# Attention products of two tiles at a time, in quarters of the array, in a fused attention and MLP kernel

## The chip, the cores and the metric

The kernel runs on one core of a Trainium2 chip. TensorE (PE in the profile) multiplies matrices out of on-chip memory into PSUM, which has eight banks. VectorE (DVE) and ScalarE (ACT) do elementwise work and read and write PSUM too; SyncE (SP) issues the DMAs. Each engine takes its instructions strictly in the order in which the program lists them, and waits at one whose inputs or whose buffer aren't ready; everything behind it on that engine waits too. The metric is the device time of one execution in microseconds (us); lower is better.

## The reference

Eight batches, eight heads, 576 rows, head size 64, all fp32. An attention without softmax, normalized by its root mean square for each head, then a two-layer MLP with a squared relu:

```python
kv  = np.einsum('bhsd,bhse->bhde', k, v)
out = np.einsum('bhsd,bhde->bhse', q, kv)
rms = np.sqrt(np.mean(out * out, axis=-1, keepdims=True) + 1e-06)
x   = (out / rms * g_norm)            # (B,H,S,D) -> (B*S, H*D): 4608 x 512
h   = x @ w_in                        # 512 x 2048
g   = np.maximum(h, 0.0) ** 2
y   = g @ w_out                       # 2048 x 512
```

The MLP is nearly all of the arithmetic. For each row the attention needs a product with a 64x64 matrix for each head.

## The kernel before

**Tiles and strips.** The 4608 rows of x are 36 tiles of 128. Two batches make nine tiles (`PAIR`): four of the even batch, one that holds the last 64 rows of both, four of the odd batch. Four tiles are a strip; nine strips, 0 to 8, are worked one after the other. `x_n[n]` is the normalized tile n, `xt[s]` the transposed strip, which feeds the MLP.

**The MLP.** The products of a strip are written as Strassen products (seven in place of eight block products). A strip's first half, `up`, has 28 steps: four groups g, each with products in the order 1, 2, 6, 5, 7, 3, 4. Each step is 8 records of L552 on TensorE. Results gather in three kinds of PSUM banks: A (two buffers) for 1, 6, 7, 4, B for 5, 3 and C for 2. After 1, 6 and 5 ACT copies the bank aside (`snap`, L562); product 6 goes on in the bank of product 1, product 7 in that of 6, product 4 in that of 7, and product 3 in that of 5, so each waits until the bank has been read. After 2, 7 and 3 DVE adds the snap to the bank and squares the relu (L611, L612); in strips 0 and 1 product 3 is followed by two more sums (`sums_g`, L579 and L241). After 4 ACT squares the relu. The second half, `down`, has 14 steps; from strip 2 on each product of it is itself a small Strassen product (L736). Strip 0 uses plain products in its first half (`up_first`, L588), beside which ACT and DVE convert the fp64 weights that arrive piece by piece (L203 to L224).

**Attention work.** It is cut into slices, kept in one list (`slices`, L487 to L512), which is what fixes its order. For each batch b: for each pair p of heads `transposed_query` and `key_value`, then for each tile `query` and, one place behind, `features` (batch 1) or `squares_x` (batches 2 to 7). `attend(n)` (L515) issues all slices up to place n. In strip s it is called after every step, with a place that grows in a straight line from `ready[s]` to `ready[s+1]` while the step weights (1 for a step of `up`, 2 for one of `down`, 56 in a strip from strip 2 on) reach 0.42 of their sum, so all slices of a strip fall into the first 24 steps of `up`. In strip 0 the slices of batch 1 fall one each on the last eight steps of `up_first` and the first six steps of `down`. Batch 0 comes ahead of everything, in `first_queries`, `first_normalized` and `first_features`.

- `key_value` (L342): 20 records on TensorE; the two heads of a pair stand in two halves of the array's columns. ACT copies the two 64x64 results into the diagonal of a 128x128 matrix `kvd[b, p]` with zeros elsewhere (L351, L352).
- `products_x` (L365): a query tile times `kvd`, four products of 128x128x128 into one bank; the mixed tile takes two halves of columns (L373).
- `mean_squares` and `inverse_root` (L381, L390): ACT squares the bank into `sq` (one buffer), DVE sums over each head and scales, ACT takes a root, DVE a reciprocal and one Newton step in three small instructions; `normalized` multiplies.
- `features` (L448): TensorE transposes a copied tile. `squares_x` (L456): DVE transposes squares of 32x32 straight out of PSUM, then SP stores to DRAM and loads four times into `xt`.
- PSUM: `apsum` has four buffers with the tag `at` for all of the attention, taken in turn; A, A, B, C have the other four banks.

Of the kernel before, what the change touches and what calls it, by code (L numbers as in the profile page):

```python
# [9 lines left out]
FP32 = mybir.dt.float32  # L10
# [3 lines left out]
AF = mybir.ActivationFunctionType  # L14
ALU = mybir.AluOpType
AX = mybir.AxisListType
# [3 lines left out]
def kernel(  # L20
# [34 lines left out]
    nc = tc.nc  # L55
    P = 128
    B, H, S, D = q.shape
    n_tok = B * S
    d_model = H * D
    d_ff = moe_w_in.shape[1]  # L60
    NP = H // 2
    FC = d_ff // P
    C = S // P
    REST = S - C * P
    PAIR = 2 * C + 1
    assert 2 * REST == P
    N_TILE = n_tok // P
    NT = 4
# [6 lines left out]
    X_ON_PE = 2  # L75
# [6 lines left out]
    xn_pool = ctx.enter_context(tc.tile_pool(name="xn", bufs=2))  # L82
# [4 lines left out]
    conv = ExitStack()  # L87
    raw_pool = conv.enter_context(tc.tile_pool(name="raw", bufs=8))
    wtmp = conv.enter_context(tc.tile_pool(name="wtmp", bufs=4))
    apsum = ctx.enter_context(tc.tile_pool(name="apsum", bufs=4, space=bass.MemoryType.PSUM))  # L90
    fpsum = ctx.enter_context(tc.tile_pool(name="fpsum", bufs=1, space=bass.MemoryType.PSUM))
    ctx.enter_context(tc.manual_schedule())

# [268 lines left out]

    by_head = lambda t: t.rearrange("p (h d) -> p h d", d=D)

    def products_x(n):  # L365
        m, c = divmod(n, PAIR)
        ps = apsum.tile([P, d_model], FP32, name="x_ps", tag="at")
        for p in range(NP):
            o = ps[:, ts(p, P)]
            if c == C:  # L370
                for h in range(2):
                    half = slice(REST * h, REST * (h + 1))
                    nc.tensor.matmul(  # L373
                        o[half], lhsT=qT["rest", m, p][:, half], rhs=kvd[2 * m + h, p], start=True, stop=True
                    )
            else:
                b, c_b = (2 * m, c) if c < C else (2 * m + 1, c - C - 1)
                nc.tensor.matmul(o, lhsT=qT[b, p][:, c_b, :], rhs=kvd[b, p], start=True, stop=True)  # L378
        return ps

    def mean_squares(ps):  # L381
        n = ps.shape[-1] // D
        sq = xn_pool.tile([P, d_model], FP32, name="sq", tag="sq", bufs=1)
        nc.scalar.activation(sq, ps, AF.Square)
        ms = small.tile([P, H], FP32, name="ms", tag="ms")
        nc.vector.reduce_sum(out=ms, in_=by_head(sq), axis=AX.X)
        nc.vector.tensor_scalar(out=ms, in0=ms, scalar1=1.0 / D, scalar2=EPS, op0=ALU.mult, op1=ALU.add)
        return ms

    def inverse_root(ms):  # L390
        r = small.tile([P, H], FP32, name="rms", tag="rms")
        nc.scalar.activation(r, ms, AF.Sqrt)
        nc.vector.reciprocal(r, r)

        t = small.tile([P, H], FP32, name="newton", tag="newton")
        nc.vector.scalar_tensor_tensor(out=t, in0=ms, scalar=-0.5, in1=r, op0=ALU.mult, op1=ALU.mult)
        nc.vector.tensor_tensor(out=t, in0=t, in1=r, op=ALU.mult)
        nc.vector.scalar_tensor_tensor(out=r, in0=t, scalar=1.5, in1=r, op0=ALU.add, op1=ALU.mult)
        return r

    def normalized(n, ps, r):

        on_pe = n < X_ON_PE * C + (X_ON_PE > 1)
        x_n[n] = xn_pool.tile([P, d_model], FP32, name="x_n", tag="x_n") if on_pe else ps
        nc.vector.tensor_tensor(
            out=by_head(x_n[n]), in0=by_head(ps), in1=r.unsqueeze(2).to_broadcast([P, H, D]), op=ALU.mult
        )

    def query(n):
        ps = products_x(n)  # L410
        normalized(n, ps, inverse_root(mean_squares(ps)))

    first = {}

    def first_queries(p):

        ps = apsum.tile([P, NT, P], FP32, name="x_ps", tag="at")
        for n in range(NT):
            nc.tensor.matmul(ps[:, n, :], lhsT=qT[0, p][:, n, :], rhs=kvd[0, p], start=True, stop=True)
        steps = conversion(p, w_in[:, p % KH, 0, p // KH * 2 : p // KH * 2 + 2])  # L420
        next(steps)
        next(steps)
        first[p] = flat(ps), mean_squares(flat(ps)), steps

    def first_normalized(p):
        ps, ms, steps = first.pop(p)
        next(steps)
        x_n["first", p] = t = xn_pool.tile([P, NT, P], FP32, name="x_n", tag="x_n")
        r = inverse_root(ms)
        nc.vector.tensor_tensor(  # L430
            out=by_head(flat(t)), in0=by_head(ps), in1=r.unsqueeze(2).to_broadcast([P, H, D]), op=ALU.mult
        )
        for _ in steps:
            pass

    def first_features(p):
        t, x = x_n.pop(("first", p)), open_xt(0)
        ps = apsum.tile([P, NT, P], FP32, name="xt_ps", tag="at")
        for n in range(NT):
            nc.tensor.transpose(ps[:, n, :], t[:, n, :], ident)  # L440
        nc.scalar.activation(x[:, :, p, :], flat(ps).rearrange("p (a t) -> p a t", t=SQ), AF.Copy, scale=g_col)
# [14 lines left out]
    def squares_x(n):  # L456

        s, i = divmod(n, NT)
        t, x = x_n.pop(n), open_xt(s)
        q = xn_pool.tile([P, 4, NP, SQ], FP32, name="x_q", tag="x_n")  # L460
        nc.vector.transpose(
            out=q.rearrange("p f q t -> p q f t"), in_=t.rearrange("p (q f d) -> p q f d", q=NP, f=4)
        )
        d = dram.tile([P, 4, NP, SQ], FP32, name="x_d", tag="x_d", bufs=4)
        nc.sync.dma_start(out=d, in_=q)
        for f in range(4):
            nc.sync.dma_start(
                out=x[ts(f, SQ), ts(i, 4)].rearrange("d a q t -> d a (q t)"),
                in_=d[:, f].rearrange("(a d) q t -> d a (q t)", a=4),
            )  # L470
# [17 lines left out]
    for b in range(B):  # L488
        for p in range(NP):
            if b:  # L490
                slices += [(transposed_query, (b, p)), (key_value, (b, p))]
                continue

            slices += [(convert_on_act, (p,)), (transposed_query, (b, p)), (key_value, (b, p))]
            if p > 0:
                slices.append((first_normalized, (p - 1,)))
            slices.append((first_queries, (p,)))
            if p > 0:
                slices.append((first_features, (p - 1,)))
        first_n = b // 2 * PAIR + (C if b % 2 else 0)  # L500
        ns = list(range(first_n, first_n + C + b % 2))
        if b == 0:
            slices += [(first_normalized, (NP - 1,)), (first_features, (NP - 1,))]
            ready[0] = len(slices)
            continue
        for i in range(len(ns) + 1):
            if i < len(ns):
                slices.append((query, (ns[i],)))
            if 0 < i <= len(ns):
                slices.append((features if b < X_ON_PE else squares_x, (ns[i - 1],)))  # L510
            if i > 0 and ns[i - 1] % NT == NT - 1:
                ready[ns[i - 1] // NT] = len(slices)  # L512
    slice_at = [0]

    def attend(n):  # L515
# [374 lines left out]
```

## Time and profile before

| what | us |
|---|---|
| median of 6 runs | 963.99 (963.38 to 964.73) |
| the profiled execution | 964.27 |
| its span in the trace | 962.5 |
| TensorE busy, matmul records | 928.5 (5976 records) |
| DVE busy | 644.4 |
| ACT busy | 229.0 |
| L378 x_ps, whole query tiles | 29.5 busy, 224 records |
| L373 x_ps, mixed tiles | 4.4 busy, 64 records |

A row of instruction groups gives the line, engine, operation, what is written and read, the shape and the number of records. One fp32 product appears as two records of matmul and two of weight load (PEld). A matmul record's duration includes the pipeline, and records overlap: what counts for the time is how far one start lies behind the other. The chain that ended last is followed back from the last instruction, at each step to what released it.

### The profile page before, as it was taken

The numbers are of one execution on the slowest core, as the hardware profiler recorded it, in microseconds if no ns is written. First come the engines' busy times: TensorE is split into PE (matmuls) and PEld (weight loads), VectorE is DVE, ScalarE is ACT, GpSimd is POOL, SyncE is SP. The second block draws the span as 40 slices with busy tenths as digits, with TensorE's granted clock in tenths as the row PEclk, the third lists the DMA queues.
The fourth block names the chain that finished last, engine by engine and source line by source line (L and its number), as shares of the span: only waits on it lengthen the run. The fifth ranks groups of instructions, "written<-read, shape, count | busy, mean of one in ns | idle before, by whom it ended". The sixth has DMA issues, their size and how long they took to land.

```text
span 962.5 us, 15319 instructions
## 1 busy us (share of the span) xinstructions
PE 928.5 (96%) x5976; PEld 816.7 (85%) x5976; DVE 644.4 (67%) x1161; ACT 229.0 (24%) x501; POOL 1.7 (0%) x7
## 2 busy tenths in 40 slices
PE   3699999999999999999999999999999999999996
PEld 3344888888888998899989998999889988998996
DVE  3899764585437875587648874786568655863583
ACT  3697441320023002210222012201320022002200
POOL 0000000000000000000000000000000000000000
PEclk9899999999999999999999999999999999999998
DMA  8699883636974585557564765467506721672064
GB/s 243 223 291 302 271 224 137 141 100 217 321 244 124 176 290 173 124 178 258 191 153 129 254 217 155 119 227 274 134 23 239 251 91 55 229 256 63 15 233 147
DMA packets 164520, 180.33 MB, mean 187 GB/s; under 512 B 85088, under 2 KB 138848, under 8 KB 155872
## 3 DMA queue, kind: packets, MB, share of 16 engines
q1 hardware_dynamic: 164288, 179.36, 59.0%
q8 instruction: 47, 0.77, 0.3%
q14 instruction: 25, 0.20, 0.1%
q10 hardware_dynamic: 160, 0.00, 0.0%
HBM read 148.11 MB, written 31.20 MB: 186 GB/s over the span
## 4 chain that ended last, share of the span: by engine, by line
PE 95%; ACT 2%; DVE 2%; DMA 1%; SPq 0%; issue 0%; DVEq 0%
PE ps_A L552 29%; PE ps_B L552 14%; PE ps_B L736 14%; PE ps_A L736 14%; PE ps_C L552 12%; PE ps_A L588 3%; PE x_ps L378 3%; PE kv_ps L349 2%; PE ps_B L588 1%; PE ps_C L588 1%; DMA raw<-in_moe_w_in_dram 1%; PE x_ps L373 0%; ACT raw L206 0%; ACT w_c L203 0%; PE xt_ps L440 0%
## 5 line engine op out<-in xcount | busy, mean ns | idle before, releaser
L552 PE MATMUL ps_A<-x_t,w_in 128*128 128x256 f32 x768 | 182.6, 381 | 1.3 <-DVE gt L611 1.3
L552 PEld LDWEIGHTS ps_A<-x_t,w_in 128*128 128x128 f32 x768 | 143.6, 190 | 21.1 <-DVE gt L611 2.1
L736 PE MATMUL ps_B<-w_blk,g_s 128*128 128x128 f32 x672 | 81.9, 275 | 0.0
L736 PE MATMUL ps_A<-w_blk,g_s 128*128 128x128 f32 x672 | 81.9, 275 | 0.0
L736 PEld LDWEIGHTS ps_B<-w_blk,g_s 128*128 128x128 f32 x672 | 78.4, 192 | 0.0
L736 PEld LDWEIGHTS ps_A<-w_blk,g_s 128*128 128x128 f32 x672 | 78.4, 192 | 0.0
L612 DVE SCALAR_TENSOR_TENSOR gt<-gt 128x512 f32<-128x512 f32 x96 | 66.4, 692 | 3.3
L562 ACT COPY snap<-ps_A 128x512 f32<-128x512 f32 x68 | 39.8, 585 | 113.8 <-PE ps_A L552 93.2
L611 DVE TENSOR_TENSOR gt<-ps_C,snap 128x512 f32<-128x512 f32 x32 | 22.0, 688 | 65.0 <-PE ps_C L552 65.0
L736 PE MATMUL ps_B<-w_blk,gt 128*128 128x128 f32 x504 | 63.1, 275 | 0.0
L736 PE MATMUL ps_A<-w_blk,gt 128*128 128x128 f32 x504 | 63.1, 275 | 0.0
L611 DVE TENSOR_TENSOR gt<-ps_A,snap 128x512 f32<-128x512 f32 x32 | 22.0, 688 | 60.0 <-PE ps_A L552 59.9
L552 PE MATMUL ps_A<-xT,w_in 128*128 128x256 f32 x256 | 61.2, 382 | 0.0
L552 PE MATMUL ps_C<-xT,w_in 128*128 128x256 f32 x256 | 61.0, 381 | 0.0
L552 PE MATMUL ps_B<-x_t,w_in 128*128 128x256 f32 x256 | 60.9, 381 | 0.0
L241 DVE TENSOR_TENSOR gt<-gt 128x2048 f32<-128x2048 f32 (+1 forms) x31 | 58.1, 1873 | 4.0 <-PE ps_C L552 3.8
L552 PE MATMUL ps_B<-xT,w_in 128*128 128x256 f32 x256 | 60.7, 380 | 0.0
L736 PEld LDWEIGHTS ps_A<-w_blk,gt 128*128 128x128 f32 x504 | 60.2, 192 | 0.4
L736 PEld LDWEIGHTS ps_B<-w_blk,gt 128*128 128x128 f32 x504 | 60.2, 192 | 0.4
L552 PE MATMUL ps_C<-w_blk,gt 128*128 128x256 f32 x256 | 56.6, 379 | 0.0
L552 PEld LDWEIGHTS ps_C<-xT,w_in 128*128 128x128 f32 x256 | 48.2, 190 | 6.7 <-issue 0.2
L552 PEld LDWEIGHTS ps_B<-xT,w_in 128*128 128x128 f32 x256 | 48.3, 190 | 6.5
(118 smaller groups left out, 1263.5 us busy)
## 6 DMA issues: line engine op xcount, KB each, us to landing
w_blk<-w_deep SPq DMA_DIRECT2D x42, 1024.0 KB, 5.3
w_blk<-w_out SPq DMA_DIRECT2D x42, 768.0 KB, 4.9
w_blk<-w_out SPq DMA_DIRECT2D x18, 1024.0 KB, 5.1
raw<-in_moe_w_in_dram SPq DMA_DIRECT2D x16, 512.0 KB, 6.5
raw<-in_moe_w_out_dram SPq DMA_DIRECT2D x16, 512.0 KB, 5.4
k<-in_k_dram SPq DMA_DIRECT2D x30, 256.0 KB, 2.9
v<-in_v_dram SPq DMA_DIRECT2D x30, 256.0 KB, 3.6
w_deep<-w_t SPq DMA_DIRECT2D x7, 1024.0 KB, 8.7
```

What stands on the lines that cost most here:

```text
L241: eng.tensor_tensor(out=out, in0=a, in1=b, op=ALU.subtract)
L349: nc.tensor.matmul(ps[ts(h, D)], lhsT=a, rhs=w, start=c == 0, stop=c == C)
L378: nc.tensor.matmul(o, lhsT=qT[b, p][:, c_b, :], rhs=kvd[b, p], start=True, stop=True)
L552: nc.tensor.matmul(bank[BANK[p]][:, i, :], lhsT=lhsT(k), rhs=rhs(k), start=p in (1, 5, 2) and i == 0 and k == 0, stop=k == n - 1, skip_gro ...
L562: nc.scalar.copy(snap[p], b)
L588: nc.tensor.matmul(ps, lhsT=w_in[:, kc % KH, g, kc // KH * 2 + fh, ts(i, P)], rhs=xt[0][:, :, kc, :], start=kc == 0, stop=kc == NP - 1,)
L611: nc.vector.tensor_tensor(out=o, in0=b, in1=a, op=ALU.add)
L612: nc.vector.scalar_tensor_tensor(out=o, in0=o, scalar=0.0, in1=o, op0=ALU.max, op1=ALU.mult)
L736: nc.tensor.matmul(chain[c][x][:, i, :], lhsT=a[:, f, :], rhs=w[:, f, :], start=p not in (6, 7, 3) and j in (1, 3) and f == 0, stop=f == F ...
```

## The change

`products_x` takes two tiles at once (the last tile of an odd batch alone). Every product is cut into four of 64x64x64: the rows of the array by the head's parity r, its columns by the halves of the tile's rows. So only the two nonzero 64x64 blocks of `kvd` are used. Even heads go into one bank, odd heads into another; tile i takes half of each bank. This two-bank tile has one buffer, tag `x`; `at` goes from four buffers to two, and the first queries and first features move into banks A, B and C.

`query` now holds the products and the mean squares of both tiles; `normalized` is a slice of its own with one root and one Newton step for both; then come the two `features` or `squares_x`. `squares_x` transposes in two instructions, one for each bank. With the longer list the slices move: tile 8's query goes from strip 0 into strip 1, and `ready` changes.

```diff
-    apsum = ctx.enter_context(tc.tile_pool(name="apsum", bufs=4, space=bass.MemoryType.PSUM))
+    apsum = ctx.enter_context(tc.tile_pool(name="apsum", bufs=2, space=bass.MemoryType.PSUM))
...
-    def products_x(n):
-        m, c = divmod(n, PAIR)
-        ps = apsum.tile([P, d_model], FP32, name="x_ps", tag="at")
+    def products_x(ns):
+
+        ps = apsum.tile([P, 2, 2, d_model // 2], FP32, name="x_ps", tag="x", bufs=1)
         for p in range(NP):
-            o = ps[:, ts(p, P)]
-            if c == C:
+            for i, n in enumerate(ns):
+                m, c = divmod(n, PAIR)
                 for h in range(2):
                     half = slice(REST * h, REST * (h + 1))
-                    nc.tensor.matmul(
-                        o[half], lhsT=qT["rest", m, p][:, half], rhs=kvd[2 * m + h, p], start=True, stop=True
-                    )
-            else:
-                b, c_b = (2 * m, c) if c < C else (2 * m + 1, c - C - 1)
-                nc.tensor.matmul(o, lhsT=qT[b, p][:, c_b, :], rhs=kvd[b, p], start=True, stop=True)
+                    if c == C:
+                        q, b = qT["rest", m, p], 2 * m + h
+                    else:
+                        b, c_b = (2 * m, c) if c < C else (2 * m + 1, c - C - 1)
+                        q = qT[b, p][:, c_b]
+                    for r in range(2):
+                        row = slice(D * r, D * (r + 1))
+                        nc.tensor.matmul(
+                            ps[half, r, i, ts(p, D)], lhsT=q[row, half], rhs=kvd[b, p][row, row], start=True, stop=True
+                        )
         return ps
 
-    def mean_squares(ps):
-        n = ps.shape[-1] // D
-        sq = xn_pool.tile([P, d_model], FP32, name="sq", tag="sq", bufs=1)
-        nc.scalar.activation(sq, ps, AF.Square)
-        ms = small.tile([P, H], FP32, name="ms", tag="ms")
-        nc.vector.reduce_sum(out=ms, in_=by_head(sq), axis=AX.X)
+    def mean_squares(parts):
+        ms = small.tile([P, 2, H], FP32, name="ms", tag="ms")[:, : len(parts)]
+        for i, ps in enumerate(parts):
+            sq = xn_pool.tile(list(ps.shape), FP32, name="sq", tag="sq", bufs=1)
+            nc.scalar.activation(sq, ps, AF.Square)
+            if len(ps.shape) == 3:
+                sq = sq.rearrange("p r e -> p (r e)")
+            nc.vector.reduce_sum(out=ms[:, i], in_=by_head(sq), axis=AX.X)
         nc.vector.tensor_scalar(out=ms, in0=ms, scalar1=1.0 / D, scalar2=EPS, op0=ALU.mult, op1=ALU.add)
         return ms
 
     def inverse_root(ms):
-        r = small.tile([P, H], FP32, name="rms", tag="rms")
+        r, t = (small.tile([P, 2, H], FP32, name=n, tag=n)[:, : ms.shape[1]] for n in ("rms", "newton"))
         nc.scalar.activation(r, ms, AF.Sqrt)
         nc.vector.reciprocal(r, r)
 
-        t = small.tile([P, H], FP32, name="newton", tag="newton")
         nc.vector.scalar_tensor_tensor(out=t, in0=ms, scalar=-0.5, in1=r, op0=ALU.mult, op1=ALU.mult)
         nc.vector.tensor_tensor(out=t, in0=t, in1=r, op=ALU.mult)
         nc.vector.scalar_tensor_tensor(out=r, in0=t, scalar=1.5, in1=r, op0=ALU.add, op1=ALU.mult)
         return r
 
-    def normalized(n, ps, r):
-
-        on_pe = n < X_ON_PE * C + (X_ON_PE > 1)
-        x_n[n] = xn_pool.tile([P, d_model], FP32, name="x_n", tag="x_n") if on_pe else ps
-        nc.vector.tensor_tensor(
-            out=by_head(x_n[n]), in0=by_head(ps), in1=r.unsqueeze(2).to_broadcast([P, H, D]), op=ALU.mult
-        )
-
-    def query(n):
-        ps = products_x(n)
-        normalized(n, ps, inverse_root(mean_squares(ps)))
+    queried = []
+
+    def query(ns):
+        ps = products_x(ns)
+        parts = [ps[:, :, i] for i in range(len(ns))]
+        queried.append((parts, mean_squares(parts)))
+
+    def normalized(ns):
+        parts, ms = queried.pop()
+        r = inverse_root(ms)
+        for i, n in enumerate(ns):
+            by_pair = lambda t: t.rearrange("p r (q d) -> p r q d", d=D)
+            x = by_pair(parts[i])
+
+            x_n[n] = parts[i]
+            if n < X_ON_PE * C + (X_ON_PE > 1):
+                x_n[n] = xn_pool.tile([P, d_model], FP32, name="x_n", tag="x_n")
+                o = x_n[n].rearrange("p (q r d) -> p r q d", r=2, d=D)
+            else:
+                o = x
+            w = r[:, i].rearrange("p (r q) -> p r q", r=2).unsqueeze(3).to_broadcast([P, 2, NP, D])
+            nc.vector.tensor_tensor(out=o, in0=x, in1=w, op=ALU.mult)
 
     first = {}
 
     def first_queries(p):
 
-        ps = apsum.tile([P, NT, P], FP32, name="x_ps", tag="at")
+        ps = fpsum.tile([P, NT, P], FP32, name="x_ps", tag="A", bufs=2)
         for n in range(NT):
             nc.tensor.matmul(ps[:, n, :], lhsT=qT[0, p][:, n, :], rhs=kvd[0, p], start=True, stop=True)
         steps = conversion(p, w_in[:, p % KH, 0, p // KH * 2 : p // KH * 2 + 2])
         next(steps)
         next(steps)
-        first[p] = flat(ps), mean_squares(flat(ps)), steps
+        first[p] = flat(ps), mean_squares([flat(ps)]), steps
 
     def first_normalized(p):
         ps, ms, steps = first.pop(p)
         next(steps)
         x_n["first", p] = t = xn_pool.tile([P, NT, P], FP32, name="x_n", tag="x_n")
-        r = inverse_root(ms)
+        r = inverse_root(ms)[:, 0]
         nc.vector.tensor_tensor(
             out=by_head(flat(t)), in0=by_head(ps), in1=r.unsqueeze(2).to_broadcast([P, H, D]), op=ALU.mult
         )
@@ -435,7 +451,7 @@
 
     def first_features(p):
         t, x = x_n.pop(("first", p)), open_xt(0)
-        ps = apsum.tile([P, NT, P], FP32, name="xt_ps", tag="at")
+        ps = fpsum.tile([P, NT, P], FP32, name="xt_ps", tag="BC"[p % 2])
         for n in range(NT):
             nc.tensor.transpose(ps[:, n, :], t[:, n, :], ident)
         nc.scalar.activation(x[:, :, p, :], flat(ps).rearrange("p (a t) -> p a t", t=SQ), AF.Copy, scale=g_col)
@@ -458,9 +474,11 @@
         s, i = divmod(n, NT)
         t, x = x_n.pop(n), open_xt(s)
         q = xn_pool.tile([P, 4, NP, SQ], FP32, name="x_q", tag="x_n")
-        nc.vector.transpose(
-            out=q.rearrange("p f q t -> p q f t"), in_=t.rearrange("p (q f d) -> p q f d", q=NP, f=4)
-        )
+        for r in range(2):
+            nc.vector.transpose(
+                out=q[:, ts(r, 2)].rearrange("p f q t -> p q f t"),
+                in_=t[:, r].rearrange("p (q f d) -> p q f d", q=NP, f=2),
+            )
         d = dram.tile([P, 4, NP, SQ], FP32, name="x_d", tag="x_d", bufs=4)
         nc.sync.dma_start(out=d, in_=q)
         for f in range(4):
@@ -503,13 +521,12 @@
             slices += [(first_normalized, (NP - 1,)), (first_features, (NP - 1,))]
             ready[0] = len(slices)
             continue
-        for i in range(len(ns) + 1):
-            if i < len(ns):
-                slices.append((query, (ns[i],)))
-            if 0 < i <= len(ns):
-                slices.append((features if b < X_ON_PE else squares_x, (ns[i - 1],)))
-            if i > 0 and ns[i - 1] % NT == NT - 1:
-                ready[ns[i - 1] // NT] = len(slices)
+        for i in range(0, len(ns), 2):
+            slices += [(query, (ns[i : i + 2],)), (normalized, (ns[i : i + 2],))]
+            for n in ns[i : i + 2]:
+                slices.append((features if b < X_ON_PE else squares_x, (n,)))
+                if n % NT == NT - 1:
+                    ready[n // NT] = len(slices)
     slice_at = [0]
 
     def attend(n):
```

## The prediction

> **What bounds the kernel.** First the page: busy time, the slices, the chain that ended last.
>
> ```profile
> PE 928.5 (96%) x5976; PEld 816.7 (85%) x5976; DVE 644.4 (67%) x1161; ACT 229.0 (24%) x501; POOL 1.7 (0%) x7
> ...
> PE   3699999999999999999999999999999999999996
> ...
> PE 95%; ACT 2%; DVE 2%; DMA 1%; SPq 0%; issue 0%; DVEq 0%
> ```
>
> After the first 75 us TensorE has no idle tenth, and it is 95% of the chain. Microseconds taken from TensorE's stream come off the end; every new wait on TensorE is added to it. DVE and ACT matter only where TensorE stands for them.
>
> Second, the timeline of strip 2 shows what the attention products cost. Each row is one burst; the second number is its length, and a record lasts about 0.22 to 0.27 us of which most is pipeline, so I divide length minus one record by the intervals.
>
> ```profile
> 289.18 0.69 PE L349 MATMUL kv_ps<-v,k 128*64 128x64 f32 x16
> ...
> 291.84 1.09 PE L373 MATMUL x_ps<-kv_all,qT_rest 128*64 128x128 f32 x16
> ...
> 296.42 1.05 PE L378 MATMUL x_ps<-kv_all,qT 128*128 128x128 f32 x8
> ```
>
> L378, a whole tile: 4 products, 8 records, (1.05-0.275)/7 = 0.111 us each, 0.89 a tile. L373, the mixed tile: two column halves, (1.09-0.273)/15 = 0.0545 each, that is 0.109 for two together: the halves run side by side. L349, 64 columns: (0.69-0.222)/15 = 0.031 on average; two start together, and a pair of halves comes every 0.058.
>
> Third, the chain in order of time gives the length of whole strips. Each of these rows starts a strip's second half.
>
> ```profile
> 318.26 6.25 PE ps_B L736 x56
> ...
> 418.32 6.25 PE ps_B L736 x56
> ...
> 719.17 6.25 PE ps_B L736 x56
> ...
> 816.42 6.25 PE ps_B L736 x56
> ...
> 909.19 6.25 PE ps_B L736 x56
> ```
>
> The last stretch, up to the second half of strip 8, has no attention work: 909.19-816.42 = 92.77. The stretch up to 418.32 (strip 3) takes 100.06; the 7.29 extra are four key-value products and four whole query tiles, so one key-value product is (7.29-4x0.89)/4 = 0.93. Its 20 records need 20x0.029 = 0.58. The other **0.35 us is the price of going into the split array and back**. The stretch of strip 7 takes 97.25: 4.48 extra for three whole tiles (2.67). The missing 1.8 is seen here:
>
> ```profile
> 770.50 0.91 PE x_ps L378 x8
> ...
> 772.06 0.70 DVE ms L386
> ...
> 774.13 0.70 DVE x_ps L405
> 774.84 0.60 DVE gt L611
> ...
> 775.48 3.72 PE ps_A L552 x16
> ```
>
> A query right after product 5 puts its whole norm on DVE ahead of L611 of product 7, which product 4 (same bank) needs: TensorE waits 0.9, twice in this strip.
>
> **Products in quarters.** Of the 32 tiles outside the first strip, 28 cost 0.89 and 4 cost 16x0.0545+0.35 = 1.22: 29.8 us now. Afterwards each tile has 16 products of 64x64x64, 32 records, 8 groups of four. The trace has no row halves. Cheapest: four run together at the pace of L349's pair, 0.058 a group. Dearest: the row halves follow one another, 0.117. The Trainium skill speaks against the change twice. "TensorEngine Tiling (Array Packing)", Instruction Overhead, says that every matmul has some 60 cycles of overhead and that a dimension already small is not to be cut; "TensorE: Matmul & The Clock Gate" (Wait — 56ns, not 53.3ns?) puts start to start at no less than about 25 ns. By that floor 1024 records need 25.6 us; by the row they need 256x0.0584 = 14.9. L349's average of 29 ns does not break the floor, but its records start in twos a few ns apart (two per 58 ns), which fits a limit per part of the array better than one per instruction; the second page's Part 3 has 16 parts at 10.6 times the speed of one. I take the row, 14.9, and keep 25.6 and 29.9 as ends. The 18 query calls (14 pairs, 4 single tiles) each pay 0.35: 6.3, against 4 calls before. New total 21.2, **gain 8.6**.
>
> **Strip 7.** There the single tile 35 comes after product 5, but only its reduce stands ahead of L611 now (square, reduce, scale: 1.5 us after the query, L611 is due at 2.0), and the pair 33/34 comes after product 3. Both waits go: **gain 1.8**.
>
> **Two banks instead of four for transposes and key-value products.** In strips 2 and on only key-value products use them, microseconds apart: nothing. In the start the first queries move to other banks, already free: nothing. While batch 1 is brought in beside strip 0, transposes, rest transposes and key-value products alternate in two banks. Then a rest transpose needs the key-value bank before last:
>
> ```profile
> 95.26 0.68 ACT L203 ACTIVATE w_c<-raw 128x512 f32<-128x512 f32 x1 [4.17 <-DMA raw<-in_moe_w_out_dram]
> ...
> 96.86 0.27 PE L337 MATMUL tr_ps<-ident,q_rest 128*128 128x128 f32 x1
> ...
> 99.22 0.19 ACT L351 COPY kv_all<-kv_ps 64x64 f32<-64x64 f32 x1
> 99.42 0.21 ACT L352 COPY kv_all<-kv_ps 64x64 f32<-64x64 f32 x1
> ```
>
> ACT, held up by a weight piece, frees that bank at 99.63, while L337 runs at 96.86 today. TensorE would stand **2.8 us** with strip 0's products behind it, and ACT's relu behind those. An earlier wait of 0.75 (product at 83.8, copy until 84.5) is swallowed by it. Ends: 0 if the piece lands early, 3.6.
>
> **One buffer for the pair.** A pair's bank is free after DVE's transposes of its second tile, and the next query stands at the head of TensorE. I placed the slices by the due-time rule: only five queries come one step (1.73 us of TensorE) after the last transpose of the pair before. DVE rows: reduce 0.69, scale 0.17, reciprocal to third Newton step 0.82, multiply 0.70, L611 and L612 1.4 together, transpose of half a tile about 0.42 (the price of other 256-wide rows; two in a row 0.78). ACT: square 0.60. The second square waits for the first reduce, since `sq` has one buffer.
>
> Worst is strip 1, group 2. TensorE resumes after the query of 9/10 at 0: reduces end 2.7; ACT's snap of product 6 goes first, then the root at 3.1; Newton 4.0; both multiplies 5.35; L611/L612 of product 7 6.9; transpose of tile 9 7.7; product 3's two 9.0; the two sums of strip 1 (L579, L241) 10.5; transposes of tile 10 11.3. Query 11/12 is due at 8.7: wait **2.6**. Same walk without the sums: strip 2, group 2: **0.7**; strip 5, tiles 24/25 to 26: **1.0** (0.1 of it L611 late for product 4). Strips 3 and 6: transposes of one tile behind L611/L612 of product 2, done 2.5, query due 1.8: **0.7** each. One more: tile 8 moves to strip 1's start, and `features` follows one step after `normalized`; the multiply ends 4.4, TensorE is there at 3.5: **1.0**. Behind each wait stand the next step's products, then the snaps and sums that read them. Elsewhere I find product 4 and product 7 on time. Sum 6.7; bounds 0 (DVE early everywhere) and about twice that.
>
> **Norms together, transposes in two.** Fourteen chains of small operations less (1.2 us of DVE each), one instruction more per transposed tile (0.07): DVE time is covered by TensorE except in the walks above, which contain it. DMAs: the same five per tile on SP; two stores now stand closer, and SP waits for each landing, but x is wanted only at the strip's end: nothing.
>
> **Sum.** Gains 8.6+1.8 = 10.4; losses 2.8+6.7 = 9.5; net -0.9. The profiled execution took 964.27 (span 962.5 and 1.8 around): 963.4. It is 0.28 above the median of the runs, 963.99, so the forecast for the median is **963.1**.
>
> **Rivals.**
> 1. *Row halves in turn, or a floor on starts* (slower). The place is each group of four. Since my net is only -0.9 over 256 groups, it turns slower from 0.062 us a group on. At the floor 0.100: 973.8; at 0.117: 978.1. For: no row halves in the trace. Against: the column halves' behaviour. 0.17.
> 2. *The buffer waits don't bind*: DVE is ahead, only the bank wait stays: 956.4. For: DVE 67% busy. Against: strip 7, where DVE does make TensorE wait. 0.12.
> 3. *The waits are twice as long*, since a late L611 then holds product 4 too: 969.8. For: the copies and multiplies read two banks, an access that this trace doesn't show. 0.13.
>
> My own case has 0.58, with a range of 960 to 966.5.
>
> **Range and chances.** Below rival 2 I leave little; rival 1 stays outside: 955 to 971. A measurement of this kernel tells about 0.2% from no change (1.9 us, 962.1 to 965.9). Of my case I give a third to faster, under a half to same, a fifth to slower. With the rivals: faster 0.32, same 0.27, slower 0.41.
>
> **What would show it.** 64 records of a pair in about 1.2 us with records 15 ns apart (28 if rival 1); the stretches of strips 3 and 4 a little shorter; the stretch of strip 7 94.9 instead of 97.25; TensorE idle ahead of x_ps put down to L461's transposes, five times, longest in strip 1; ahead of tr_ps to ACT's L352, near 97 us; ahead of xt_ps to the multiply once. I am wrong if a group takes over 0.07, or if waits appear at queries that I passed over.

## The result and the profile after

The changed kernel takes **967.15 us** in the median of 17 runs (964.87 to 971.42). The kernel before, run beside it, took 964.31 in 38 runs. The ratio is **1.003, with a 95% interval of 1.0021 to 1.0038**: slower by 0.3%. The forecast was 963.1, no change, in a range of 955 to 971.

The profiled execution of the changed kernel happened to be one of its shortest: 964.46, span 962.3. A second execution of the same kernel, profiled later, took a span of 966.1, and the two differ in what turns out to matter. First the page of the changed kernel: busy times and the number of records, the slices of TensorE, its granted clock in the same slices, the chain that ended last.

```profile
PE 923.5 (96%) x6712; PEld 806.1 (84%) x6712; DVE 635.6 (66%) x1118; ACT 226.5 (24%) x487; POOL 1.7 (0%) x7
...
PE   3699999989999999999999999999999999999996
...
PEclk9799999999999999999999999999999999999999
...
PE 91%; DVE 4%; ACT 2%; DMA 1%; issue 1%; SPq 0%; DVEq 0%; ACTq 0%
```

TensorE has 736 records more and 5 us less busy time: the products became cheaper. But the chain has turned. Before, 95% of it was TensorE and 2% DVE; now it is 91% and 4%, and where DVE is on it TensorE stands, that is, waits and does nothing. The ninth slice of TensorE, 192 to 216 us, which was a 9, is an 8.

The timeline of strip 1 shows both sides. Each row is one burst: start, length, line, tiles, shape, records, and in brackets how long the engine stood before it and for whom.

```profile
190.44 1.16 PE L380 MATMUL x_ps<-kv_all,qT 64*64 64x64 f32 x64
...
198.54 1.89 PE L569 MATMUL ps_A<-x_t,w_in 128*128 128x256 f32 x8
202.85 1.39 PE L380 MATMUL x_ps<-kv_all,qT 64*64 64x64 f32 x64 [2.42 <-DVE x_q L478]
204.16 3.40 PE L569 MATMUL ps_A<-xT,w_in 128*128 128x256 f32 x8
```

A pair of tiles takes 1.16 us: with 0.218 for one record, (1.16-0.218)/63 = 0.015 us from record to record, four for 0.060. The quarters run four side by side, as forecast. The third row is the longest of the forecast buffer waits, 2.42. The fourth is what the forecast did not have: an ordinary MLP step of eight records, 1.89 elsewhere, takes **3.40** right behind that wait. The clock that the trace shows as granted to TensorE from 203.6 to 207.0 is one half of the full one. So the wait costs its 2.4 us and about another 1.7 = 3.4/2.

The waits of TensorE, with the time in all, the number and the longest (PEld is its weight load, which is held up by the same wait):

```profile
PE x_ps L380 <- DVE x_q L478: 4.9, 5, 2.4
...
PE tr_ps L337 <- ACT kv_all L352: 1.3, 1, 1.3
...
PEld xt_ps L469 <- DVE x_n L427: 1.2, 1, 1.2
...
PEld ps_A L569 <- DVE gt L628: 0.4, 1, 0.4
```

Five waits for the pair's buffer, one for the bank of a key-value product, one for tile 8's multiply: the predicted ones; no other new wait of a product is as long as 0.5 in this trace. The last row is what is left of the two waits of strip 7 (they appear once more in the run with two banks alone, below).

Last the chain in order of time: each of these rows, except the first, starts a strip's second half.

```profile
88.62 6.88 DMA raw<-in_moe_w_out_dram
...
321.84 6.25 PE ps_B L753 x56
...
421.06 6.25 PE ps_B L753 x56
...
520.13 6.25 PE ps_B L753 x56
...
621.18 6.25 PE ps_B L753 x56
...
720.86 6.25 PE ps_B L753 x56
...
815.75 6.25 PE ps_B L753 x56
...
908.52 6.25 PE ps_B L753 x56
```

The stretches between them, less those of before, are -0.84 for strip 3 (99.22 against 100.06), -1.33, +0.99, -0.71 and, for strip 7, 94.89 against 97.25: -2.36. Together these five give back 4.25 us. The loss is ahead of them: strip 2's second half starts at 321.84 instead of 318.26, 3.58 late. And the first row is new on the chain: a weight piece's transfer, which held up ACT, and through it the bank that TensorE waited for.

A smaller loss lies at the other end. SyncE issues the last 24 stores of the output, first before, then after the change:

```profile
949.35 11.00 SPq L657 DMA_DIRECT2D out_dram<-o_sb  x24
...
948.68 11.49 SPq L674 DMA_DIRECT2D out_dram<-o_sb  x24
```

From the start of the last second half to the end of the span it is 53.3 us before and 53.7 after, so of the 4.25 us gained nearly 0.5 is lost again here. And the device time is longer than the span by 2.15 us in the mean of 18 executions, by 1.80 in 39 of the kernel before. Both are in the second trace too (0.65 and 2.2). Why the stores are issued more slowly, and what lies outside the span, was not looked into.

### The profile page after: what moved, and what is told of

It is laid out like the page before. It is cut to its first block, busy times and chain, and to the rows that moved or that the text cites. A ratio compares the mean times of both kernels' runs of the same rounds, so it can differ in the third digit from the quotient of the medians.

```text
span 962.3 us, 16706 instructions
## 1 busy us (share of the span) xinstructions
PE 923.5 (96%) x6712; PEld 806.1 (84%) x6712; DVE 635.6 (66%) x1118; ACT 226.5 (24%) x487; POOL 1.7 (0%) x7
## 4 chain that ended last, share of the span: by engine, by line
PE 91%; DVE 4%; ACT 2%; DMA 1%; issue 1%; SPq 0%; DVEq 0%; ACTq 0%
PE ps_A L569 28%; PE ps_B L753 14%; PE ps_A L753 14%; PE ps_B L569 14%; PE ps_C L569 12%; PE ps_A L605 2%; PE kv_ps L349 2%; PE x_ps L380 2%; PE ps_C L605 1%; PE ps_B L605 1%; DMA raw<-in_moe_w_out_dram 1%; DMA raw<-in_moe_w_in_dram 1%; DVE gt L629 1%; DVE x_q L478 1%; ACT raw L206 1%
## 5 line engine op out<-in xcount | busy, mean ns | idle before, releaser
L569 PEld LDWEIGHTS ps_A<-xT,w_in 128*128 128x128 f32 x256 | 48.5, 194 | 6.9
L569 PEld LDWEIGHTS ps_B<-x_t,w_in 128*128 128x128 f32 x256 | 48.2, 190 | 6.7
```

Source lines behind the costliest of these rows:

```text
L569: nc.tensor.matmul(bank[BANK[p]][:, i, :], lhsT=lhsT(k), rhs=rhs(k), start=p in (1, 5, 2) and i == 0 and k == 0, stop=k == n - 1, skip_gro ...
```

## The experiments

The theory after the result: the sums of the forecast hold, but a wait of TensorE of some 2.4 us or more can be followed by 3.4 us at half clock, for which the forecast has no term; and the bank wait, which ends when a transfer lands, varies from one execution to the next. The first rival: the products in quarters cost more than the timeline shows. The second: DVE's or ACT's own work got dearer, and the waits only show it. The third: the half clock has nothing to do with the waits.

### Both kernels once more

> The kernel before once more, for a second trace of it. In the traces of the four experiments TensorE waited 1.3 to 2.8 us in strip 1's second half for weight blocks (w_blk) that were loaded late; the first trace of the kernel before has no such wait. If those waits belong to every kernel here and only vary from execution to execution, this trace may show them too, and the ratio is 1.000. If they come from the change's order of transfers, this trace has none. No wait of tr_ps and no half-speed stretch past 60 us in either case.

> The changed kernel once more, for a second trace; the first one was 2.7 us below the median of its runs. Theory: the bank wait is longer here (3 to 5 us instead of 1.5), or weight blocks come late in strip 1's second half, or both; the five waits for the pair's buffer are the same to 0.1 us, and the half-speed stretch after strip 1's 2.4 us wait is there again. Ratio 1.002 to 1.004.

The kernel before: 964.06 us, ratio 1.0002 (0.9992 to 1.0011), so the comparison itself adds nothing. The changed kernel: 968.32 in 5 runs, ratio 1.0044 (1.0025 to 1.0064). Its timeline, around the bank wait of strip 0 and the buffer wait of strip 1:

```profile
95.71 0.68 ACT L203 ACTIVATE w_c<-raw 128x512 f32<-128x512 f32 x1 [4.70 <-DMA raw<-in_moe_w_out_dram]
...
99.81 0.21 ACT L352 COPY kv_all<-kv_ps 64x64 f32<-64x64 f32 x1
...
100.07 0.48 PE L337 MATMUL tr_ps<-ident,q_rest 128*128 128x128 f32 x1 [2.51 <-ACT kv_all L352]
100.34 4.93 PE L605 MATMUL ps_C<-xT,w_in 128*128 128x512 f32 x8
...
205.72 1.98 PE L380 MATMUL x_ps<-kv_all,qT 64*64 64x64 f32 x64 [2.41 <-DVE x_q L478]
```

ACT stands 4.70 us for a weight piece, here, against 3.12 in the first trace of this kernel; so the bank comes free later and TensorE stands 2.51 instead of 1.30. And now half clock follows here too: eight records of `up_first`, which take 3.60 otherwise, take 4.93. The buffer wait in strip 1 is the same to 0.01 us, and is again followed by half clock (the 64 records take 1.98 instead of 1.16). Strip 0's second half starts 4.70 us later than in the first trace of before in this execution (105.93 against 101.23), and 1.82 in the other one (103.05). That is 2.9 of the 3.8 us by which the two traces of this kernel differ.

### The bank wait taken away

```diff
-            ps = apsum.tile([P, P], FP32, name="tr_ps", tag="at")
+            ps = apsum.tile([P, P], FP32, name="tr_ps", tag="x", bufs=1)
```

The rest transposes of strip 0 go through the pair's banks, which are unused there, so they need no bank of a key-value product.

> The rest transposes of batch 1 use the pair's banks, which are idle then, so that transposes and key-value products alternate in two banks without meeting a bank that ACT has not yet freed. Theory (the wait for that bank ends when a weight piece lands, and differs from execution to execution): the median falls by about 4.5 us to about 962.5, below the kernel before, and the spread of the runs shrinks to that of the kernel before; no wait of tr_ps on L352 is left. Rival (the wait is the same 1.5 us in every run, and the rest of the loss lies in the pair's buffer and the clock): the median falls by 1.5 us to about 965.6 and the spread stays.

965.04 us in the median of 13 runs, ratio to before 0.9999 (0.9988 to 1.0009): 0.31 points, **3.0 us, below the changed kernel**. Its waits:

```profile
PE x_ps L380 <- DVE x_q L478: 4.9, 5, 2.4
...
PE ps_B L569 <- DMA w_blk<-w_out: 1.5, 1, 1.5
...
PE kv_ps L349 <- ACT kv_all L352: 0.7, 1, 0.7
```

The wait of tr_ps is gone. A smaller one of the next key-value product, 0.7, has come in its place, since that product needs the same copies of ACT. The buffer waits are untouched. The 3.0 us are more than the 1.3 that the first trace has for this wait, and less than the 4.5 that were expected; nor did the spread shrink as expected (961.91 to 965.96). They fit the wait of a usual execution with part of the half clock behind it, which no trace of this edit shows by itself.

### The buffer waits taken away

```diff
                 if n % NT == NT - 1:
                     ready[n // NT] = len(slices)
+            if b >= X_ON_PE and i + 2 < len(ns):
+                slices.append((lambda: None, ()))
```

An empty slice ahead of every further query of a batch gives DVE one more step of TensorE before the pair's banks are wanted again.

> An empty slice stands between the last transposes of a pair and the next query of the same batch (batches 2 to 7), so the next query comes two or three steps later and no longer waits for the pair's buffer; the bank wait stays. Theory (five waits of 5.7 us together, and the 2.4 us wait in strip 1 halves TensorE's clock for 3.4 us, which costs another 1.7): the median falls by 6 to 7.5 us, to about 960.5, the spread stays wide, and no half-speed stretch is left in strip 1. Rival (the clock falls by itself, not for that wait): the fall is 5 us at most and the half-speed stretch is still there. Rival (the added slices move other work into worse places): the fall is under 3 us.

962.88 us in 20 runs, ratio 0.9981 (0.9970 to 0.9992): **4.7 us below the changed kernel**. No wait for L478 is left, and no half clock in strip 1. The waits that remain or are new:

```profile
PE kv_ps L349 <- DMA v<-in_v_dram: 1.8, 1, 1.8
...
PE ps_B L571 <- DMA w_blk<-w_out: 1.7, 1, 1.7
...
PE tr_ps L337 <- ACT kv_all L352: 0.5, 1, 0.5
```

So the edit gains less than the 4.9 of the waits and the 1.7 behind them, and less than the 6 to 7.5 expected. TensorE, moved, meets a load of v in strip 2 that lands 1.8 us late, and that row is in no kernel without the empty slices. Half clock followed it in this execution. The bank wait is 0.5 here, with the code of strip 0 unchanged: the third length that it has shown. DVE and ACT are busy for 634.8 and 226.5 us, as in the changed kernel (635.6 and 226.5), and less than before (644.4 and 229.0): the second rival falls.

### Both

> Both edits: rest transposes in the pair's banks and an empty slice ahead of the tight queries. If the two costs are separate, the falls add up: about 10 to 12 us below the changed kernel, 955 to 957, and the spread is that of the kernel before. If the bank wait costs only 1.5 us in every run, 958 to 959.5.

961.47 us in 9 runs, ratio **0.9966 (0.9953 to 0.9979)**: faster than both kernels, and 6.2 us below the changed one, where 10 to 12 were expected. Its waits:

```profile
PE kv_ps L349 <- DMA v<-in_v_dram: 1.9, 1, 1.9
PE ps_B L571 <- DMA w_blk<-w_out: 1.5, 1, 1.5
...
PE ps_A L571 <- DVE gt L630: 0.9, 1, 0.9
```

By the terms of the forecast this kernel, left with the wait of tile 8 alone, should gain 10.4-1.0 = 9.4; its trace gains 2.9 (span 959.6). The three rows hold 4.3 of the missing 6.5: two loads, and in strip 5 a wait for the squared relu, which the buffer wait had stood in front of. Of the other 2.2, 0.9 lie at the end (54.2 us from the start of the last second half, 53.3 before), and 0.7 is a second wait for ACT's snap (1.4 in two, 0.7 in one before). The last 0.6 is not placed. A stand of TensorE that is taken away uncovers the next thing that was nearly late.

### Two banks alone

```diff
-    apsum = ctx.enter_context(tc.tile_pool(name="apsum", bufs=4, space=bass.MemoryType.PSUM))
+    apsum = ctx.enter_context(tc.tile_pool(name="apsum", bufs=2, space=bass.MemoryType.PSUM))
...
-        ps = apsum.tile([P, d_model], FP32, name="x_ps", tag="at")
+        ps = apsum.tile([P, d_model], FP32, name="x_ps", tag="x")
```

This is the kernel before, whole products and all, but with two banks for transposes and key-value products, and two others for queries (and for the first queries and first features).

> The kernel before with one part of the change alone: transposes and key-value products share two banks, queries and first features have the other two. Theory: slower than the kernel before by 3 to 5 us, with a wider spread, from the same wait of tr_ps on L352. Rival (a constant wait): slower by 1.5 us with the same spread. If the queries had needed more than two banks, further waits on x_ps would show; none is expected.

968.0 us in 7 runs, ratio 1.0036 (1.0024 to 1.0049). Its waits:

```profile
PEld ps_A L552 <- DVE gt L611: 2.1, 2, 1.0
...
PE tr_ps L337 <- ACT kv_all L352: 1.3, 2, 1.0
PE ps_B L552 <- DMA w_blk<-w_out: 1.3, 1, 1.3
...
PE x_ps L378 <- DVE x_q L461: 0.4, 1, 0.4
```

Strip 0's second half starts 1.52 us late, with no half clock past the first 60 us: the bank waits alone, when they are short. The first row holds the two waits of strip 7, which this kernel still has as the kernel before did. The third, a block of `w_out` that lands late in strip 1, is in neither trace of before; with the 0.4 of a second such wait it is 1.7 of the 4.2 us that this trace is late at strip 2. The last row, a query that waits for its bank in strip 1, was not expected. Nor was the spread: wider was expected, and the seven runs lie within 1.6 us. Whether the late block belongs to the edit is taken up further down.

### Quarters or column halves

```diff
-                            ps[half, r, i, ts(p, D)], lhsT=q[row, half], rhs=kvd[b, p][row, row], start=True, stop=True
+                            ps[half, r, i, ts(p, D)], lhsT=q[:, half], rhs=kvd[b, p][:, row], start=True, stop=True
```

All 128 rows of the array work on each product, the zero block of `kvd` included, with two column halves side by side: everything of the change but the row halves.

> The changed kernel with the row halves given up: every product takes all 128 rows (the zeros of kvd included) and only the columns are halved, the same number of instructions and records. If the four quarters run side by side and a group of four takes 0.058 us as in the trace, this gives groups of twice two: 0.117 a group, a pair 2.2 us instead of 1.28, 15 us more over 256 groups, about 982 us. If the row halves gained nothing, the time is that of the changed kernel, 967.

982.4 us in 4 runs, ratio 1.0186 (1.0158 to 1.0214): 15 us above the changed kernel, 14 above its runs beside this one. The timeline of a pair in strip 1:

```profile
193.56 2.13 PE L380 MATMUL x_ps<-kv_all,qT 128*64 128x64 f32 x64
```

(2.13-0.22)/63 = 0.030 a record, 0.121 for four. 256 groups of four times (0.121-0.060) are 15.6, and the runs have 14 to 15. The first rival falls: the row halves are worth what the forecast said, and the quarters carry no hidden price.

### A stand of TensorE, put in on purpose

```diff
+    def pause(n):
+        z, d = (apsum.tile([P, P], FP32, name=name, tag="at") for name in ("z_ps", "d_ps"))
+        x = xn_pool.tile([P, d_model], FP32, name="wait", tag="sq", bufs=1)
+        nc.tensor.transpose(z, ident, ident)
+        nc.vector.tensor_copy(x[:, 0:P], z)
+        for _ in range(n):
+            nc.vector.memset(x, 0.0)
+        nc.vector.memset(d, 0.0)
+        nc.tensor.transpose(d, ident, ident)
+        nc.vector.tensor_copy(x[:, 0:P], d)
...
+            if s >= DEEP and i == 24:
+                pause(2)
```

To the kernel before, and so with none of the change in it, one stand is added in each of strips 2 to 8: TensorE transposes into a tile that DVE must fill first. With n = 0, 2 and 5 the stand gets longer. Only work is added.

> The kernel before with a deliberate stand of TensorE once in each of strips 2 to 8, after product 5 of the last group: it waits for a DVE copy, two fills of 512 elements and a small fill, some 1.6 us; 7 stands. Theory (a stand over about 2 us halves TensorE's clock for 3.4 us, a shorter one doesn't): about 7 times 2.0 us with the two transposes, 978, and no half-speed stretch past 60 us. Rival (any stand can lower the clock): half-speed stretches here too.

987.33 us, ratio 1.0236. The stands became longer than meant, 1.9 to 2.6 us. Timeline, strips 2 and 3:

```profile
317.82 0.33 PE L803 MATMUL d_ps<-ident 128*128 128x128 f32 x1 [2.23 <-DVE d_ps L802]
317.99 2.52 PE L552 MATMUL ps_A<-x_t,w_in 128*128 128x256 f32 x8
320.30 2.99 PE L552 MATMUL ps_B<-xT,w_in 128*128 128x256 f32 x8
...
422.25 0.33 PE L803 MATMUL d_ps<-ident 128*128 128x128 f32 x1 [2.23 <-DVE d_ps L802]
422.41 1.89 PE L552 MATMUL ps_A<-x_t,w_in 128*128 128x256 f32 x8
```

The same stand of 2.23 us: behind one the next two steps take 2.52 and 2.99, behind the other 1.89. Half clock for 3.4 us came behind **2 of the 7**; those two stretches of a strip grew by 4.5 and 4.4 us, the other five by 2.3 to 3.0. Two further lengths follow.

> The same deliberate stand of TensorE as in the run with two extra fills, once in each of strips 2 to 8 of the old kernel, but with no extra fill, so that each stand is about 1.3 us (two fills made 2.2 to 2.9, so one fill is about 0.5). Theory (a stand of about 2.4 us and more can be followed by 3.4 us at half clock, one well below is not): no stretch at half clock anywhere past the first 60 us, every one of the seven strip stretches longer by the same 1.3 to 2 us (stand and the two transposes), together about +10 to +14 us, ratio 1.010 to 1.015. Rival (half clock follows the phase of the run and not the length of the stand): again one or two of the seven stands with half clock behind it, as with two fills.

974.77 us, ratio 1.0109 (1.0089 to 1.0128). Timeline, strip 3:

```profile
417.56 0.33 PE L803 MATMUL d_ps<-ident 128*128 128x128 f32 x1 [0.92 <-DVE d_ps L802]
417.73 1.89 PE L552 MATMUL ps_A<-x_t,w_in 128*128 128x256 f32 x8
```

Stands of 0.6 to 1.0 us, and half clock behind **none of the 7**. From strip 3 on the stretches are longer by 1.0 to 1.4 us, the stand and its two transposes.

> The same stand with five extra fills: about 3.5 to 4.2 us each (two fills: 2.2 to 2.9). Theory (the longer the stand past about 2.4 us, the surer the half clock behind it): half clock for 3.4 us behind at least five of the seven stands, each of them 1.7 us dearer than the stand itself; the seven stretches longer by about 4 us without it and about 5.7 with it, together +34 to +42 us, ratio 1.035 to 1.044. Rival (half clock follows the phase of the run): again one to three of seven, ratio about 1.030 to 1.034.

1009.88 us, ratio 1.0477 (1.0459 to 1.0494), a little above what was expected. Timeline, strip 3:

```profile
425.21 0.33 PE L803 MATMUL d_ps<-ident 128*128 128x128 f32 x1 [4.20 <-DVE d_ps L802]
425.38 3.40 PE L552 MATMUL ps_A<-x_t,w_in 128*128 128x256 f32 x8
```

Stands of 3.9 to 4.3 us, and half clock behind **all 7**: five times for 3.4 us and twice for 6.8. That is 30.7 us at half clock, 15.4 lost; with the 31.3 us for which the weight loads stood it makes 46.7, and the trace is 45.8 us longer than that of before. The mean granted clock of the span is 0.977, against 0.994 before.

The third rival falls here. In a kernel without the change, stands of up to 1.0, 1.9 to 2.6 and 3.9 to 4.3 us are followed by half clock in 0, 2 and 7 of 7 cases.

What decides between two equal stands can be read from the same traces. In each trace the changes of the granted clock lie whole multiples of 3.413 us apart (here 319.11 and 629.72: 91 times). So the span can be cut into windows on that grid. Each row for n = 2 gives such a window, its length, TensorE's busy time with the number of records, and the granted clock:

```profile
315.69:319.10 3.41, 1.28 (x7) 1.00 0.21 77
319.11:322.52 3.41, 3.41 (x10) 0.50 0.26 76
...
418.09:421.50 3.41, 1.93 (x10) 1.00 0.33 90
421.51:424.92 3.41, 2.67 (x13) 1.00 0.36 121
...
520.49:523.90 3.41, 2.59 (x13) 1.00 0.28 79
523.91:527.32 3.41, 1.67 (x8) 1.00 0.27 95
```

The stand of 2.23 us in strip 2 lies nearly whole in one window, which is idle for 2.13 us; the next window runs at half clock. The equal stand of strip 3 falls across two windows, idle for 1.48 and 0.74, and nothing happens. The longest stand of this run, 2.58 us in strip 4, is also split (0.82 and 1.74) and has no half clock behind it. The kernel with column halves shows the same for a wait of the change itself:

```profile
206.90 2.10 PE L380 MATMUL x_ps<-kv_all,qT 128*64 128x64 f32 x64 [2.38 <-DVE x_q L478]
...
205.04:208.45 3.41, 1.55 (x53) 1.00 0.32 96
208.46:211.87 3.41, 3.41 (x33) 1.00 0.18 62
```

It waits 2.38 us for the pair's buffer in strip 1, of which 1.86 fall into one window, and the clock stays. From 60 us to the end of the products the 13 traces have some 3400 windows. At full clock, 14 of them are followed by half clock, and these are idle for 1.80 to 3.41 us; of all the others none is idle for more than 1.86. In the two stretches of 6.8 us, another 1.56 and 0.88 us of the stand fell into the first half-clock window. The idle times come from the matmul records, whose ends are modelled, and no run moved a stand against the grid on purpose.

These runs bear on the late blocks of `w_out` as well. The first and the second of them (n = 2 and 0) wait 2.5 and 1.7 us for `w_blk` in strip 1, where their instructions are still those of the kernel before; the third waits 0.2. So that wait can come without the change. Whether the change makes it more frequent, and why the blocks land late in some executions, is open.

### Tile 8 too

```diff
+            if b < X_ON_PE and i + 1 == len(ns):
+                slices.append((lambda: None, ()))
             for n in ns[i : i + 2]:
```

> The kernel with both mends (rest transposes in the pair's bank, an empty slice ahead of each further query of a batch), with one more empty slice between tile 8's normalization and its features. Theory: the wait of xt_ps for the multiply of x_n near the start of strip 1 (0.8 to 1.2 us in the changed kernel) goes and nothing else changes: about 1 us below the kernel with both mends, ratio to the kernel before 0.9950 to 0.9965. Rival: the shift of the other slices by one place costs as much: 0.9966, as with both mends.

960.39 us in 9 runs, ratio **0.9959 (0.9944 to 0.9973)**. The wait of xt_ps at L469 is gone from the trace, and the span is 958.8. It is the fastest version here, but its interval overlaps that of the version with both mends alone, so this last step is shown by the wait in the trace and not by the times.

## Why the prediction was wrong

**Products in quarters: right.** The forecast took 0.058 us for a group of four, by the pace of column halves, against the two pages cited there, which spoke for 0.1 or more. It measured 0.060, and the column halves alone cost 14 to 15 us more. The first rival is refuted.

**Strip 7: right.** Forecast 94.9 for the stretch, measured 94.89.

**One buffer for the pair: right in place, number and length.** Five waits, none at another query, 4.9 us in all on TensorE; forecast 2.6+0.7+1.0+0.7+0.7 = 5.7, the longest 2.6 against 2.42. Strips 3 to 7 came out within 0.2 us each of the forecast's terms: together these make -4.2 (products -4.8, strip 7's waits -1.8, buffer waits +2.4), and both traces have -4.25. Rival 2 (they don't bind) falls; so does rival 3, twice as long.

**Tile 8's features: right.** 1.0 forecast, 0.8 on TensorE and 1.2 on its weight loads.

**Norms, transposes, DMAs at nothing: right inside the strips**, as far as the trace shows: TensorE waits for none of the five stores and loads of a tile. The 0.5 us of the last stores and the 0.35 outside the span are terms that the sum did not have.

**Where the sum failed: each wait of TensorE was priced at its length alone.** The sentence "TensorE would stand **2.8 us** with strip 0's products behind it" names the right wait, with the right releaser and place; so does "wait **2.6**" for strip 1. But a stand of that length has a price beyond itself, which **the sum had no term for**: half clock for 3.4 us, 1.7 us more. The bank wait's length, besides, is no constant: it ends when a transfer lands, and in four traces with this code in strip 0 it was 0.5, 1.3, 1.6 and 2.5 us.

With this term the sum fits both traces of the changed kernel up to the second half of strip 2, for which the rest of its -0.9 is +3.3. In the short execution strip 0's last rest transpose comes 1.8 us late instead of 2.8 (98.62 against 96.86), one half-clock stretch follows the wait in strip 1, and the waits of the pair's buffer and of tile 8 are 0.5 shorter than forecast: 3.3-1.0+1.7-0.5 = 3.5; measured 3.58. In the long one that transpose comes 3.2 late, two stretches cost 1.5 and 1.7, and `w_out` is 0.5 late: 3.3+0.4+1.5+1.7+0.5-0.5 = 6.9; measured 7.29.

Over all runs the mean granted clock says the same: 0.9909 in the 23 executions of the changed kernel on record, 0.9930 in 81 of the one before. (Both means include the half clock at the start and at the end, which every trace has.) The difference of 0.0021 times 965 is **2.1 us**, with a 95% interval of 1.3 to 2.8: one half-clock stretch more for each execution, or a little over. The forecast was 3.8 us below 966.9, which is 1.003 times the median before. The clock is about half of that, the end of the kernel and the time outside the span some 0.9. The rest, about 1 us and no more than the uncertainty of the clock's part, is not settled.

That the time lies inside the stated range, and that slower had the largest of the three chances, 0.41, is no merit of the argument: most of that chance came from rivals 1 and 3, which the runs refute.

**The rule that the forecast should have weighed.** The Trainium skill, "TensorE: Matmul & The Clock Gate" (Part 1, on the two states), says that the array falls to half clock after an idle window of about 3.4 us and that these windows run freely; the page's table of goals asks for no gaps over about 3 us. By that, waits of 2.4 cost nothing extra; by the runs each can cost 1.7. The traces agree with the 3.4 us and with a free grid. They do not agree with the gap. Of the five buffer or bank waits of 2.4 to 2.5 us in traces of kernels with the change, four were followed by half clock, and the one with column halves was not; of the deliberate stands of 1.9 to 2.6 us, 2 of 7. The late load of v, 1.8 to 1.9 us, was followed by it in one of three kernels (with the buffer waits away, but not with both mends, nor with tile 8's too), the 1.7 and 1.5 us for `w_blk` in none. What fits all of these is the share of one window: about 1.8 of 3.41 us idle is the border, not the whole. An estimate from these numbers: a stand of 2.3 us then has a chance of (3.4+2.3-3.6)/3.4 = 0.62, one of 4.2 is sure to do it, one of 0.9 never.

## What to carry to other kernels

Price a wait of a busy TensorE by its length only while it is short; from about 1.8 us on add the chance of 3.4 us at half clock. Two waits of 1.2 us that lie well apart are then cheaper than one of 2.4 (an estimate from the windows above; no run compared them), and one cheap step of delay between a reader and the next writer of a buffer (an empty slice here) can be worth more than the wait it removes. Where a wait ends on a transfer, read its length from several executions. And after a stall is removed, look at once for what stood behind it: here two loads and a squared relu took back 4.3 us.

## What the runs showed of the hardware

- Products of 64x64x64 in fp32 run four side by side in the quarters of the array, a record every 0.015 us over a burst of 64; the same work in column halves takes 0.030 a record.
- TensorE's granted clock fell to one half for 3.4 us (sometimes 6.8) behind stands of 1.9 to 2.6 us in 2 of 7 cases, of 3.9 to 4.3 us in all seven, and of up to 1.0 us in none.
- The clock changed only on a grid of 3.413 us. At full clock, every window of it in which TensorE was idle for over 1.86 us was followed by half clock, and none with under 1.80: a stand of 2.23 us within one window did it, and the same stand across two did not.
- The same instructions waited 0, 1.7 and 2.5 us for blocks of `w_out` in strip 1, in different executions.
